# Four weight fetches, one weight split and six one-hot rows change their places in the last quarter of an attention loop

## The chip, the core and the metric
One core of one Trainium2 chip runs one program that does an attention layer and then a mixture-of-experts layer (MoE). The metric is the time of one execution in microseconds (us). TensorE is PE in the profile, VectorE is DVE, ScalarE is ACT, GpSimd is POOL, and SyncE (SP) issues most DMAs.

## The reference
Four batches, eight heads, 768 tokens, head size 64. Per token: attention to the 31 nearest keys (|distance| < 16) and to 24 block summaries of 32 keys each, in one softmax. Keys are summarised by a maximum, values by a mean.

```python
k_sum = k.reshape(B, H, nb, block, D).max(axis=3)
v_sum = v.reshape(B, H, nb, block, D).mean(axis=3)
a = softmax(concat(mask(q @ k.T / 8), q @ k_sum.T / 8 + log(32)))
attn = a @ concat(v, v_sum)
```

The MoE layer takes each token's 512 values. A gate picks one of eight experts by the largest logit; a second logit decides whether a token keeps the expert of the token before it. The output is `p[e] * (relu(x @ w1[e]) @ w2[e])`, with w1[e] 512 x 1024 and w2[e] 1024 x 512.

## The kernel before
**Attention.** Two heads make a pair, so there are 16 pairs, numbered n, four to a batch. Each pair is worked in two groups of three 128-token blocks: 32 groups, numbered G, with n = G // 2. The loop over G is written out in Python, and each engine runs its instructions in the order in which the loop emits them. Group G's scores (`s_mm`, L305 mask matmuls, then L311) come first; then the transposes of group G-2 (`t_stage`, L337, copied out by ACT at L338), the maximum and the exponentials of group G (`s_max` L319, `s_exp` L327), and the weighted sum of group G-3 (`a_mm` L348, scaled by DVE at L359 and L360).

**What GpSimd prepares.** For pair n+1, in pair n's first group, it copies the keys into overlapping windows (`windows`, L269, out `kb`) and folds the values once (`fold_v`, L254, reads the DMA-loaded tile `vt`). In pair n's second group it writes the key summaries into the same `kb` (`summaries`, L272). The scores of pair n+1 need both parts of `kb`. Then it spreads pair n's value summaries into `vw` (`spread_v`, L283).

**What is mixed in.** While attention runs, earlier batches are routed: x is transposed (L553, copied by ACT at L560), logits are made (`x_logits`, L570), and `route` works through small DVE steps with a few matmuls (L644 counts the tokens of each expert from `sc` of L640). The most wanted expert of batch 0, `e0`, is known early, and its weights are fetched during attention: eight chunks of 128 x 1024, 512 KB each, into a rotation of four `wst` buffers (`wfetch`, L1146 on SP). A chunk is split into a rounded part (ACT cast, L1150) and a remainder (`wsplit`: four GpSimd instructions at L1158, or one on DVE at L1153). Chunk 0 is split on GpSimd.

`rows` (L680 to L683) builds six one-hot 128 x 128 tiles of batch 0 on GpSimd from `lanf`; the routing of batch 0 leaves it to the loop, which calls it as `self.set0()` in group SET0.

**The order around the change.** SP issues, in one queue: in the first group of pair n the value loads `vt` of pair n+2 and `vw` of pair n+1; in the second group the keys and queries of pair n+3; weight fetches come behind the loads of their group. Near the end of each group the jobs registered for "point 1" run (L461), then `set0` (L462). The lists are read in `have_e0` (L1400 to L1405):

```python
for j in range(len(WSPLIT)):
    at(WSPLIT[j], 1, wsplit, j)
for j in range(len(WFETCH)):
    at(WFETCH[j], 1, wfetch, j)
```

Chunk 4 reuses chunk 0's buffer, so its fetch in group 26 waits for the end of split 0. After the loop, six more splits and two more fetches follow at fixed points of the tail, and the MoE work begins with the first gathered tokens (L1164, L1175).

Of the kernel before, what the change touches and what calls it, by code (L numbers as in the profile page):

```python
# [50 lines left out]
WARM = 11  # L51
WHOLE = (3, 4, 5)
LATE = (*WHOLE, 9, 13)
SET0 = 25
BEHIND = (5, 16, 24, 30)
SOON = (8, 12)
FILL = {2: 5}

WFETCH = (21, 21, 22, 22, 26, 30)
WSPLIT = (24, 29)  # L60
WBY = "GGGVVVGV"

TAIL = {0: ("t", 30), 1: ("a", 29), 2: ("t", 31), 4: ("a", 30), 5: ("a", 31)}
# [21 lines left out]
class Kernel:  # L85
# [87 lines left out]
    def attention(self, tick, rows, tail):  # L173
        nc, tc, ident = self.nc, self.tc, self.ident
        with ExitStack() as ctx:
# [200 lines left out]
            for G in range(last_g):  # L376
# [84 lines left out]
                tick(G, 1)  # L461
                if G == SET0:  # L462
                    self.set0()
# [913 lines left out]
    def run(self):  # L1377
# [5 lines left out]
        def at(G, point, f, *args):  # L1383
            jobs.setdefault((G, point), []).append((f, args))
# [6 lines left out]
        def wfetch(j):  # L1391
            w, q = divmod(j, NCH)
            st["w", j] = self.awk.tile([P, CH], F32, name="wst", bufs=4)
            self.fetch(st["w", j], w, q * CH, (q + 1) * CH, st["e0"])

        def wsplit(j):
            w, q = divmod(j, NCH)
            self.split(w, q * CH, (q + 1) * CH, st.pop(("w", j)), nc.vector if WBY[j] == "V" else nc.gpsimd)

        def have_e0():  # L1400
            st["e0"] = nc.values_load(self.e0[0:1, 0:1], engines=(ENG.SP,), min_val=0, max_val=E - 1)
# [5 lines that stand above are left out]
# [50 lines left out]
        def tail(stage):  # L1457
# [3 lines left out]
            for k in range(XL[-1] + 4):  # L1461
# [5 lines left out]
                if k in WLAST:  # L1467
                    wsplit(len(WSPLIT) + WLAST.index(k))
                if k in WLATE:
                    wfetch(len(WFETCH) + WLATE.index(k))  # L1470
                for u in range(NU):
# [289 lines left out]
```

## Time and profile before

| what | value |
|---|---|
| time, median of 3 runs | 436.49 us (434.3 to 437.31) |
| profiled execution: time, span | 433.81 us, 432.0 us |
| PE busy | 416.2 us, 96% of the span |
| DVE, ACT, POOL busy | 234.1, 197.5, 165.9 us |
| PE clock granted, mean | 0.99 of full speed |
| HBM traffic | 69.65 MB read, 12.71 MB written |

The span is what the trace covers; the time is what was measured for the execution, 1.8 us more. Attention fills about the first 115 us, the MoE layer the rest. In a timeline row the columns are start, duration, engine, line and operation, then output, inputs, shape and count; a bracket gives the idle time of that engine ahead of the row and who ended it.

### The profile page before, as it was taken

The page shows a single profiled execution, that of the slowest core. Times are in us where ns is not written, and L with a number is a line of the kernel's source. Part 1 is how long each engine was busy: PE and PEld are TensorE (multiplying, and loading weights), DVE is VectorE, ACT ScalarE, POOL GpSimd, SP SyncE. Part 2 cuts the span into 40 slices and gives each one's busy share as a digit, 9 for nine tenths or more (in the row PEclk, how much of TensorE's full clock was granted, in tenths as well). Part 3 has the DMA queues.
Part 4 walks back from the last instruction along what each step waited for, and adds up shares of the span by engine and source line. Part 5 has one row for each costly group of instructions (what it writes and reads, how often), then busy time and mean ns, then how long its engine had stood idle before and what let it go on. Part 6 is the DMA issues. An engine that isn't in the chain of part 4 may idle for free.

```text
span 432.0 us, 11296 instructions
## 1 busy us (share of the span) xinstructions
PE 416.2 (96%) x4227; PEld 360.3 (83%) x4228; DVE 234.1 (54%) x575; ACT 197.5 (46%) x466; POOL 165.9 (38%) x255
## 2 busy tenths in 40 slices
PE   7999999989999999999999999999999999999992
PEld 4787887868898798988987998799899889879781
DVE  4876796978788689957721022112435202254560
ACT  4988887967865227322121222122634212263561
POOL 3667686798624315753022103110630310321131
PEclk9999999989999999999999999999999999999997
DMA  8999999997251850394076912110257210219312
GB/s 310 403 396 402 400 329 377 401 402 284 95 177 68 325 212 0 99 368 170 2 284 231 374 52 72 29 50 0 99 185 255 90 58 0 57 53 388 105 51 58
DMA packets 22279, 83.27 MB, mean 193 GB/s; under 512 B 2702, under 2 KB 3344, under 8 KB 19120
## 3 DMA queue, kind: packets, MB, share of 16 engines
q1 hardware_dynamic: 17600, 67.75, 41.1%
q0 software_dynamic: 4448, 14.29, 10.0%
q8 instruction: 39, 0.64, 0.6%
q14 instruction: 48, 0.39, 0.3%
q10 hardware_dynamic: 144, 0.20, 0.2%
HBM read 69.65 MB, written 12.71 MB: 191 GB/s over the span
## 4 chain that ended last, share of the span: by engine, by line
issue 25%; DMA 12%; POOLq 5%; POOL 4%; PE 3%; DVE 3%; DVEq 0%
DMA out_dram<-yo,sidx 9%; POOLq L1273 4%; POOL xg L1164 2%; DMA out_dram<-few_y,sidx 2%; DMA xg<-x_dram,gidx 1%; DVE bp L1084 1%; POOL l L1158 1%; POOLq L1481 1%; PE bs L1249 1%; PE bt L1111 1%; PE bs L1251 0%; PE bs L1252 0%; DVE hT L1258 0%; DVE eqp L1078 0%; POOL out_dram L1209 0%
## 5 line engine op out<-in xcount | busy, mean ns | idle before, releaser
L1249 PE MATMUL bs<-xT,h 128*128 128x384 f32 (+1 forms) x288 | 91.3, 317 | 0.0
L1251 PE MATMUL bs<-xT,h 128*128 128x384 f32 (+1 forms) x288 | 89.8, 312 | 0.0
L1252 PE MATMUL bs<-xT,l 128*128 128x384 f32 (+1 forms) x288 | 89.7, 311 | 0.0
L1196 PE MATMUL ba<-h,hT 128*128 128x512 f32 x192 | 78.9, 411 | 1.4 <-PEq L1646 0.8
L1258 DVE SCALAR_TENSOR_TENSOR hT<-bs,hT 128x384 fp32r<-128x384 f32 (+1 forms) x56 | 33.2, 593 | 82.9 <-ACT hT L1256 69.2
L1198 PE MATMUL ba<-h,hT 128*128 128x512 f32 x192 | 75.3, 392 | 0.0
L1197 PE MATMUL ba<-l,hT 128*128 128x512 f32 x192 | 75.0, 391 | 0.0
L1256 ACT ACTIVATE hT<-bs 128x384 fp32r<-128x384 f32 (+1 forms) x56 | 29.3, 523 | 86.9 <-PE bs L1252 84.9
L1164 POOL DMA_INDIRECT xg<-x_dram,gidx x30 | 29.4, 981 | 101.5 <-PE bt L1175 90.5
L1249 PEld LDWEIGHTS bs<-xT,h 128*128 128x128 f32 x288 | 54.5, 189 | 0.8 <-issue 0.4
L327 ACT ACTIVATE pr<-bs,nm 128x120 f32<-128x120 f32 x192 | 51.7, 372 | 7.5 <-DVE nm L319 6.9
L1251 PEld LDWEIGHTS bs<-xT,h 128*128 128x128 f32 x288 | 54.5, 189 | 0.4
L1252 PEld LDWEIGHTS bs<-xT,l 128*128 128x128 f32 x288 | 54.5, 189 | 0.0
L1209 POOL DMA_INDIRECT out_dram<-yo,sidx x24 | 28.0, 1168 | 64.4 <-ACT yo L1205 40.9
L1196 PEld LDWEIGHTS ba<-h,hT 128*128 128x128 f32 x192 | 36.2, 189 | 8.7 <-issue 2.6
L1198 PEld LDWEIGHTS ba<-h,hT 128*128 128x128 f32 x192 | 36.0, 188 | 8.2
L1197 PEld LDWEIGHTS ba<-l,hT 128*128 128x128 f32 x192 | 36.2, 189 | 6.0
L1153 DVE TENSOR_TENSOR l<-stg,h 128x1024 fp32r<-128x1024 f32 x28 | 34.4, 1274 | 12.0 <-ACT h L1150 11.9
L1170 DVE TENSOR_TENSOR xT<-bt,xT 128x512 fp32r<-128x512 f32 x27 | 18.6, 691 | 36.5 <-ACT xT L1168 34.3
L1150 ACT CAST h<-stg 128x1024 fp32r<-128x1024 f32 x32 | 32.2, 1049 | 11.4 <-PEq L1646 4.6
L1205 ACT ACTIVATE yo<-ba,psort 128x512 f32<-128x512 f32 x24 | 16.5, 688 | 45.1 <-PE ba L1198 41.5
L283 POOL COPY vw<-vs 24x384 f32<-24x384 f32 x64 | 29.9, 509 | 13.6 <-ACT vs L278 5.4
(269 smaller groups left out, 639.4 us busy)
## 6 DMA issues: line engine op xcount, KB each, us to landing
stg<-in_w SPq DMA_DIRECT2D x16, 1024.0 KB, 7.7
vw<-in_vW SPq DMA_DIRECT2D x16, 780.0 KB, 7.4
few_w<-in_w SPq DMA_DIRECT2D x8, 1024.0 KB, 8.4
kp<-in_kT SPq DMA_DIRECT2D x16, 384.0 KB, 6.9
q<-in_qT SPq DMA_DIRECT2D x16, 384.0 KB, 7.6
vt<-in_vT SPq DMA_DIRECT2D x16, 384.0 KB, 7.0
x_dram<-xs SPq DMA_DIRECT2D x8, 768.0 KB, 5.8
wst<-in_w SPq DMA_DIRECT2D x8, 512.0 KB, 7.4
```

The costliest lines, as they stand in the source:

```text
L283: nc.gpsimd.tensor_copy(out=vw[n % 3][WL:W, t:t + NW // 4, :, 0:D], in_=vs.to_broadcast([NB, NW // 4, 2, D]))
L327: nc.scalar.activation(out=pr[:, h, u, 0:W], in_=sp[:, h, u, :], func=AF.Exp, bias=nm[:, h, u:u + 1], scale=1.0)
L1150: self.nc.scalar.copy(out=hi, in_=src)
L1153: eng.tensor_tensor(out=lo, in0=src, in1=hi.bitcast(F32), op=ALU.subtract)
L1164: self.nc.gpsimd.indirect_dma_start(out=t, out_offset=None, in_=rows, in_offset=bass.IndirectOffsetOnAxis(ap=self.gidx[:, i:i + 1], axis=0))
L1196: nc.tensor.matmul(out=ps, lhsT=ah, rhs=wh, start=first, stop=False)
L1197: nc.tensor.matmul(out=ps, lhsT=ah, rhs=wl, start=False, stop=False)
L1198: self.last_mm = nc.tensor.matmul(out=ps, lhsT=al, rhs=wh, start=False, stop=last).ins
L1249: ins = nc.tensor.matmul(out=ps[:, j], lhsT=wh, rhs=xh[c], start=(c == 0), stop=False).ins
L1251: nc.tensor.matmul(out=ps[:, j], lhsT=wh, rhs=xl[c], start=False, stop=False)
L1252: nc.tensor.matmul(out=ps[:, j], lhsT=wl, rhs=xh[c], start=False, stop=(c == KT - 1))
L1258: nc.vector.scalar_tensor_tensor(out=l, in0=ps, scalar=0.0, in1=h.bitcast(F32), op0=ALU.max, op1=ALU.subtract)
```

## The change
Three constants change. The first four weight chunks are fetched in groups 22, 22, 23 and 23 instead of 21, 21, 22 and 22. The one-hot rows of batch 0 are built in group 24 instead of 25. Chunk 0 is split in group 25 instead of 24. The later fetches (26, 30) and the second split (29) stay.

```diff
-SET0 = 25
+SET0 = 24
...
-WFETCH = (21, 21, 22, 22, 26, 30)
-WSPLIT = (24, 29)
+WFETCH = (22, 22, 23, 23, 26, 30)
+WSPLIT = (25, 29)
```

On GpSimd, the order from group 24 on was: windows and fold of pair 13, split 0, summaries of pair 13, spread of pair 12, one-hot rows. It becomes: windows and fold of pair 13, one-hot rows, summaries of pair 13, spread of pair 12, split 0. On ACT the cast of chunk 0 moves from the end of group 24 to the end of group 25. On SP the four fetches move past the loads of one group: chunks 0 and 1 go behind `vt` of pair 13 and `vw` of pair 12, chunks 2 and 3 behind the keys and queries of pair 14.

## Rows read from the trace of the kernel before

**Rows 1.** Windows: busy us (and instructions) by engine, PE clock, DMA share, GB/s
```profile
80.00:100.00 20.00, 17.91 (x331) 14.80 (x319) 17.05 (x41) 15.54 (x52) 15.74 (x30) 0.91 1.02 396
100.00:120.00 20.00, 20.00 (x354) 17.31 (x348) 16.01 (x52) 15.62 (x48) 13.36 (x24) 1.00 0.44 153
...
200.00:432.00 232.00, 222.46 (x1420) 198.16 (x1418) 79.58 (x127) 71.94 (x113) 48.42 (x45) 0.99 0.33 117
```

**Rows 2.** Waits of PE from 80 to 96 us: total, times, longest
```profile
PE bs L311 <- POOL kb L272: 1.9, 1, 1.9
```

**Rows 3.** Timeline of PE: starts of groups 18, 19, 26, 27; scores and logits
```profile
60.03 0.35 PE L305 MATMUL bs<-me 64*64 64x360 bf16 x4
...
63.73 0.35 PE L305 MATMUL bs<-me 64*64 64x360 bf16 x4
...
88.25 0.35 PE L305 MATMUL bs<-me 64*64 64x360 bf16 x4
90.48 0.85 PE L311 MATMUL bs<-kb,q 64*64 64x120 f32 x24 [1.88 <-POOL kb L272]
...
95.52 0.35 PE L305 MATMUL bs<-me 64*64 64x360 bf16 x4
...
100.04 1.07 PE L570 MATMUL bs<-hs,wg 128*32 128x128 f32 x24
```

**Rows 4.** Timeline of POOL, groups 24 and 25, and one row of group 29
```profile
81.30 1.49 POOL L269 TENSOR_SCALAR kb<-kp 128x384 f32<-128x384 f32 x3
84.85 1.15 POOL L254 TENSOR_TENSOR vf<-vt 128x192 f32<-128x192 f32 x2 [2.06 <-DMA vt<-in_vT]
87.25 2.78 POOL L1158 TENSOR_TENSOR l<-wst,h 128x256 fp32r<-128x256 f32 x4 [1.25 <-ACT h L1150]
89.99 0.43 POOL L272 TENSOR_SCALAR kb<-ks 128x288 f32<-128x288 f32 x1
90.49 1.85 POOL L283 COPY vw<-vs 24x384 f32<-24x384 f32 x4
92.44 3.52 POOL L682 TENSOR_SCALAR A<-c,lanf 128x128 bf16<-128x128 f32 x6
...
104.94 0.43 POOL L272 TENSOR_SCALAR kb<-ks 128x288 f32<-128x288 f32 x1 [0.56 <-DVE tl L853]
```

**Rows 5.** SP's issues; landing times of vt (pair 13), of four weight chunks
```profile
75.79 0.89 SPq L1146 DMA_DIRECT2D wst<-in_w  x2
76.79 0.38 SPq L202 DMA_DIRECT2D vt<-in_vT  x1
...
80.01 0.88 SPq L1146 DMA_DIRECT2D wst<-in_w  x2
...
DMA to landing us min/median/max: 7.9/7.9/7.9
...
DMA to landing us min/median/max: 6.7/7.8/8.9
```

**Rows 6.** Windows, the stretch behind the stall, columns as in the first group
```profile
92.00:95.30 3.30, 3.30 (x37) 3.05 (x34) 1.97 (x5) 2.76 (x9) 3.20 (x6) 0.50 1.02 399
```

**Rows 7.** Timeline of ACT, groups 24, 25 and 27
```profile
86.13 1.04 ACT L1150 CAST h<-wst 128x1024 fp32r<-128x1024 f32 x1
...
87.82 1.62 ACT L327 ACTIVATE pr<-bs,nm 128x120 f32<-128x120 f32 x6
...
97.05 0.86 ACT L338 COPY pt<-bt 124x384 f32<-124x384 f32 x2 [0.84 <-PE bt L337]
...
99.41 1.05 ACT L560 COPY hs<-bt 128x512 f32<-128x512 f32 x2
```

**Rows 8.** Timeline of DVE: routing steps of batch 1, one of batch 2
```profile
89.40 0.65 DVE L632 TENSOR_SCALAR e_all<-ev 128x6 int32<-128x6 int32 x1
...
90.51 0.59 DVE L640 TENSOR_TENSOR_SCAN sc<-c,oh 128x48 bf16<-128x48 f32 x1
...
125.65 0.16 DVE L632 TENSOR_SCALAR e_all<-ev 128x6 int32<-128x6 int32 x1
```

## The prediction
> **What bounds the kernel now.** I read the busy time by stretches first [rows 1]. From 100 us on PE is busy in all or nearly all of each stretch, while between 80 and 100 us it is busy for 17.91 of 20.00 us, its granted clock is 0.91, and the DMA engines are full (share 1.02, 396 GB/s). So the kernel is bound by PE, with a hole just where the edit lies. Next came the waits of PE there: one matters, the scores waiting for GpSimd's key summaries, 1.9 us, once [rows 2]. Then the timeline of PE around it [rows 3]: group 26 starts at 88.25, its L311 only at 90.48, and group 27 at 95.52, so group 26 lasts 7.27 us. Group 18, which has the same mixture (a pair's first group, two blocks of x transposed), lasts 63.73 - 60.03 = 3.70 us. The excess is 3.57 us, and two things make it up. The wait is 1.88. Behind it the granted clock is 0.50, the lower level of 1.2 GHz, for 3.30 us [rows 6], which costs half of that, 1.65 us. Together 3.53: the hole is explained.
>
> Last I followed GpSimd back from that wait [rows 4]. Ahead of the summaries at 89.99 stand, from the back: split 0 (2.78 us), 1.25 us of waiting for ACT's cast of chunk 0, the fold (1.15 us), and 2.06 us of waiting for the `vt` load of pair 13. That load was issued at 76.79, right behind two weight chunks at 75.79, and landed after 7.9 us, at 84.7 [rows 5].
>
> **The change, part by part.**
>
> *Fetches.* Chunks 0 and 1 go behind `vt`: 2 x 512 KB = 1.05 MB at 396 GB/s [rows 1] is 2.65 us of transfer that no longer stands ahead of it. If the queue serves in order of issue, `vt` lands near 84.7 - 2.65 = 82.05. GpSimd is free at 81.30 + 1.49 = 82.79 [rows 4], so the 2.06 us of waiting goes and the fold runs from about 82.8 to 83.95. Chunks 0 and 1 now go out where 2 and 3 did, at 80.01 and just after, and land 6.7 to 8.9 us later [rows 5], at 86.7 to 89.4. Chunks 2 and 3 move one group on; they are split only in the tail, past 115 us, which hides them. The loads passed by them land earlier or as before. Issuing costs SP the same 0.89 us per two, so its queue holds nothing new.
>
> *Rows and split on GpSimd.* In the place of the 1.25 us wait and the 2.78 us split come the six rows, 3.52 us, whose input was finished long before: 83.95 + 3.52 = 87.5, plus 0.43 for the summaries = 87.9. PE asks for them at about 88.4. The wait of 1.88 us should be gone with 0.5 us to spare, and with it the cause of the clock's fall. The spread follows (1.85 us) to 89.8, then split 0 once cast. Fetch 4 waits for split 0's end, near 93.3 instead of 90.0; it was issued only at 97 before, so SP loses nothing.
>
> *Next on GpSimd.* Split 0 ends near 90.5 + 2.78 = 93.3; windows, fold and summaries of pair 14 (1.49, 1.15, 0.43) end at 96.4. Group 28's L311 ran one L311 (0.85 us) before L570, at about 99.2 [rows 3]; 96.4 permits it 2.8 us earlier.
>
> *ACT.* The cast (1.04 us) leaves group 24 and lands behind the exponentials of group 25. Those end at 87.82 + 1.62 = 89.44 [rows 7], or up to 0.67 sooner, since the copy behind the cast could start when its transposes were done. In order from there: cast 1.04, copy 0.86, exponentials 1.62, two hs copies 1.05, copy 0.86, exponentials 1.62, a small copy of about 0.25, and half of 1.05 for the hs tile that L570 of group 28 needs. That is 7.8 us: ready at 97.3, or 96.6. Against 100.04 the gain is 2.7 to 3.4. Before, ACT idled through the stall, and that idle time hid such work; now it doesn't. PE alone would have arrived 3.57 earlier, at 96.5, so up to 0.8 us of the prize is given back here and on GpSimd; the two lie beside each other and count once.
>
> *DVE.* The routing steps before L644 end at 90.51 + 0.59 = 91.10 [rows 8]. PE used to be stalled; now it comes to L644 near 89.9. The same step L632 took 0.65 us with GpSimd working and 0.16 with it idle [rows 8]. At the short durations there is no wait; if the steps still end at 91.1, PE waits 1.2 us, group 27 starts at 93.15 and L570 at 97.7, a gain of 2.4.
>
> The Trainium skill, GPSIMD Engine Reference, section 8 (Key points), says that GpSimd shares its SBUF interfaces with VectorE and contends with DVE instructions in a two-port mode or with two SBUF inputs. By that rule the long durations stay, as GpSimd is still busy there (the spread), and the sum would be 2.4; by the idle-GpSimd row it would be 2.7 or more.
>
> *Carried to the end.* PE is busy in 20.00 of 20.00 us from 100 to 120, and in 222.46 of 232 after 200 [rows 1]; the gathers, splits and later fetches are issued by steps that follow the same loop, so they move with it. The nearest thing to a fixed date is the last pairs' loads, as the DMA engines are full until about 102 us: the last `vt` can't come 3 us earlier. But GpSimd's summaries of pair 15 at 104.94 waited for DVE and not for a load [rows 4], and they run some 2 to 3 us before group 30 asks. I carry the gain whole.
>
> *Sum.* Ends 2.4 and 3.4, I take 2.9 us: 433.81 - 2.9 = 430.9 for the profiled execution. That one lies 2.68 below the median of the three runs (436.49), so the median to expect is **433.6 us**, 0.7% less.
>
> **The rivals.**
> 1. *The load does not come earlier* (the DMA queue does not serve in order, or the load was late for another reason). For: the landing times alone don't prove an order. Against: chunks take 6.7 to 8.9 us in a full queue, growing as they queue up [rows 5]. Then the fold still ends at 86.0, the rows at 89.5, the summaries at 89.95: 0.5 us better, the stall and the low clock stay. Time 436.0. Chance 0.14. The Trainium skill, DMA: Bandwidth & Descriptors, Queues, rings and completion order, says that completion is not first-in-first-out per issuing engine, which is this rival's mechanism; no run here shows yet which holds for these loads.
> 2. *The stall goes or shrinks to under 1 us, but the clock falls anyway* in group 26 or 27, because PE still meets short waits there. It costs the 1.65 us again: gain 1.3, time 435.2. For: the fall came 1.5 us after the wait had ended. Against: at no other place of the attention did a short wait bring it. Chance 0.13.
> 3. *More than the hole:* the runs shown are 0.5 to 3.5 us longer than the profiled one; if they lose that in a longer stall at this place, the gain is about 5, time 431.5. Nothing in the profile speaks for the place. Chance 0.06.
> 4. *Slower: the cast of chunk 0 holds ACT.* ACT runs in order; it now meets the cast 3 us later, but the chunk is issued 4.2 us later. From a landing past about 89 us ACT stands still, and past 92.4 the split delays pair 14's summaries beyond the old 99.2, each us counting fully, plus 1.65 if the clock falls. A landing at 95.5 would cost 3.1 + 1.65 = 4.8, time 441. Against: it takes 15.5 us for a load where 8.9 is the longest of the four. Chance 0.05.
>
> That the lists do what they say is plain from how they are read.
>
> **How the numbers follow.** Forecast 0.62, rivals 0.14, 0.13, 0.06, 0.05. A measurement of this kernel tells about 1% from no change, 4.36 us. The forecast and rivals 1 and 2 lie within it, except where the medians scatter: the three runs span 3.0 us, which may push a gain of 2.9 past 4.36. I put 0.13 of the forecast and all of rival 3 there: faster 0.19. Slower is rival 4 and a trace of scatter, 0.06. Same 0.75. The range takes the forecast's ends (gain 2.4 to 3.4) with 2 us of scatter below, and reaches to rival 1 above: 430.8 to 436.7. The forecast's own range is 431.5 to 435.
>
> **What would show it.** L311 of group 26 without a wait for L272; granted clock 1.00 from 92 to 96; the fold of pair 13 at 82.8 with no DMA wait ahead; group 26 about 3.7 to 4.9 us long; L570 of group 28 near 97.1. Wrong would be: the fold still at 84.8 (rival 1), a 0.50 clock with no stall (rival 2), ACT idle ahead of the cast (rival 4), or a gain at group 28 that is gone by 200 us.

## The result and the profile after

The changed kernel took **431.21 us** (median of 7 runs, 430.94 to 435.22), the kernel before 435.77 (7 runs, 434.3 to 437.31). The medians lie 4.56 us apart; the ratio, which goes by all the runs, gives less: 0.9919, 95% interval [0.9892, 0.9947], 0.8% or some 3.5 us. A repetition on another chip (below, `e4_after_again`) gave 0.9927 [0.9904, 0.9951]. So it is faster by 0.7 to 0.8%, and both intervals exclude 1.

A profile shows one execution: those of the kernel before, of `e4_after_again` and of `e7` are the shortest of their kernel's runs, and the first one of the changed kernel and those of `e3`, `e6` and `e8` are the longest. So the first profile of the changed kernel (435.22 us, span 433.4) has to be read with care. Its windows show a PE that is busy for less of the stretch than before [rows 1], though the granted clock no longer falls [rows 6]:

```profile
80.00:100.00 20.00, 15.85 (x311) 13.12 (x303) 16.71 (x43) 14.96 (x50) 16.02 (x31) 1.00 0.99 365
92.00:95.30 3.30, 1.58 (x32) 1.24 (x31) 2.91 (x7) 1.25 (x4) 3.19 (x7) 1.00 1.02 393
```

The timeline of PE in it shows why. L311 follows L305 at once in group 26, as forecast; but PE now stands still twice at other places:

```profile
90.27 0.45 PE L348 MATMUL ba<-vw,pt 124*64 124x65 f32 x6 [1.94 <-issue]
90.64 0.35 PE L305 MATMUL bs<-me 64*64 64x360 bf16 x4
90.82 0.79 PE L311 MATMUL bs<-kb,q 64*64 64x120 f32 x24
94.13 0.18 PE L644 MATMUL bt<-sc,cb 128*128 128x8 bf16 x1 [1.72 <-DVE sc L640]
96.18 0.35 PE L305 MATMUL bs<-me 64*64 64x360 bf16 x4
...
100.70 1.07 PE L570 MATMUL bs<-hs,wg 128*32 128x128 f32 x24
```

The 1.94 us are put down to "issue", nothing that the profile shows. L570 of group 28 comes at 100.70, later than the 100.04 of before [rows 3]. A second profile of the same kernel, which came with `e4_after_again`, shows an execution of 430.09 us, span 428.3. All statements on the change rest on that one. Its windows:

```profile
80.00:100.00 20.00, 19.39 (x382) 15.97 (x375) 19.02 (x48) 17.73 (x58) 18.59 (x36) 1.00 1.01 377
92.00:95.30 3.30, 3.30 (x67) 2.73 (x66) 3.23 (x10) 3.08 (x10) 3.30 (x7) 1.00 0.97 357
```

PE is busy for 19.39 of 20.00 us where it was 17.91, and in the stretch that had run at half clock it issues 67 matmuls where it had issued 37. The timeline of PE, against [rows 3]:

```profile
87.62 0.35 PE L305 MATMUL bs<-me 64*64 64x360 bf16 x4
87.87 0.84 PE L311 MATMUL bs<-kb,q 64*64 64x120 f32 x24
90.14 0.18 PE L644 MATMUL bt<-sc,cb 128*128 128x8 bf16 x1 [0.61 <-DVE sc L640]
92.19 0.35 PE L305 MATMUL bs<-me 64*64 64x360 bf16 x4
95.99 0.79 PE L311 MATMUL bs<-kb,q 64*64 64x120 f32 x24
96.71 1.15 PE L570 MATMUL bs<-hs,wg 128*32 128x128 f32 x24
```

Group 26 lasts 92.19 - 87.62 = 4.57 us (7.27 before), and L570 of group 28 starts 3.33 us earlier (100.04 - 96.71). Of these, 2.70 us are made in group 26, 0.48 in group 25 (2.84 us instead of 3.32; before, PE stopped there for 0.21 us with nothing to wait for, see the last section), and 0.15 ahead of group 22. Group 27 lasts 3.63 us in both. From L570 to the end of the span it takes 428.3 - 96.71 = 331.6 us, before 432.0 - 100.04 = 332.0. So nearly the whole gain is made ahead of L570, and nothing is given back.

The timeline of GpSimd, against [rows 4]:

```profile
81.19 1.49 POOL L269 TENSOR_SCALAR kb<-kp 128x384 f32<-128x384 f32 x3
82.77 1.15 POOL L254 TENSOR_TENSOR vf<-vt 128x192 f32<-128x192 f32 x2
83.90 3.52 POOL L682 TENSOR_SCALAR A<-c,lanf 128x128 bf16<-128x128 f32 x6
87.39 0.44 POOL L272 TENSOR_SCALAR kb<-ks 128x288 f32<-128x288 f32 x1
87.88 1.85 POOL L283 COPY vw<-vs 24x384 f32<-24x384 f32 x4
89.84 2.84 POOL L1158 TENSOR_TENSOR l<-wst,h 128x256 fp32r<-128x256 f32 x4
92.64 1.47 POOL L269 TENSOR_SCALAR kb<-kp 128x384 f32<-128x384 f32 x3
94.06 1.17 POOL L254 TENSOR_TENSOR vf<-vt 128x192 f32<-128x192 f32 x2
95.18 0.45 POOL L272 TENSOR_SCALAR kb<-ks 128x288 f32<-128x288 f32 x1
...
102.28 1.15 POOL L254 TENSOR_TENSOR vf<-vt 128x192 f32<-128x192 f32 x2 [2.30 <-DMA vt<-in_vT]
```

From the windows of pair 13 to the end of the summaries of pair 14 there is hardly any idle time left: 95.63 - 81.19 = 14.44 us. Before, the same nine pieces of work took from 81.30 [rows 4] to 98.93, that is 17.63 us, with 2.06 + 1.25 = 3.31 us of waiting in them. Their end, in the kernel before:

```profile
98.50 0.43 POOL L272 TENSOR_SCALAR kb<-ks 128x288 f32<-128x288 f32 x1
```

This chain became 3.19 us shorter, and PE's way from the start of group 22 to L570 of group 28 3.18 us (23.41 to 20.23).

### The profile page after: what moved, and what is told of

The parts are those of the page before. It is cut to its first block, busy times and chain, and to the rows that moved or that the text cites. A ratio compares the mean times of both kernels' runs of the same rounds, so it can differ in the third digit from the quotient of the medians.

```text
span 433.4 us, 11296 instructions
## 1 busy us (share of the span) xinstructions
PE 414.5 (96%) x4228; PEld 359.2 (83%) x4228; DVE 234.0 (54%) x575; ACT 197.6 (46%) x466; POOL 164.4 (38%) x255
```

## The experiments

Theory: the fold's wait for `vt` (2.06 us) and the split's wait for ACT's cast (1.25 us) both stand in GpSimd's chain, and both edits are needed to take them out. The rivals: the earlier fetch alone does it; the swap alone does it; the clock's fall is what costs. The first four kernels ran together on one chip, where the kernel before had 434.80 (33 runs).

**The fetches alone** (kernel before with one line changed).

```diff
-WFETCH = (21, 21, 22, 22, 26, 30)
+WFETCH = (22, 22, 23, 23, 26, 30)
```

> Only the four fetches move (groups 22, 22, 23, 23); split 0 stays in group 24, the rows in group 25. Theory A (the stall ahead of group 26 is the sum of a late vt load and of the split with its wait for ACT, so both parts of the change are needed): vt of pair 13 lands near 82.2 and the fold is done by 84, but chunk 0 is now issued at 80.0 and lands at 86.6 to 88, so ACT stands at its cast from about 86.2, the split ends near 90.5 and the summaries near 90.9; the stall of 1.9 us stays or grows by up to 0.6: ratio to the kernel before 0.998 to 1.003. Theory B (the load of vt alone made the stall): summaries near 88, ratio 0.990 to 0.993.

Measured: 433.86 us, ratio 0.9986 [0.9971, 1.0002], no difference that can be told. GpSimd's timeline, then one row of PE's:

```profile
84.30 1.14 POOL L254 TENSOR_TENSOR vf<-vt 128x192 f32<-128x192 f32 x2 [0.95 <-DVE va L247]
...
88.66 2.77 POOL L1158 TENSOR_TENSOR l<-wst,h 128x256 fp32r<-128x256 f32 x4 [3.22 <-ACT h L1150]
91.40 0.43 POOL L272 TENSOR_SCALAR kb<-ks 128x288 f32<-128x288 f32 x1
```

```profile
91.88 1.17 PE L311 MATMUL bs<-kb,q 64*64 64x120 f32 x24 [2.40 <-POOL kb L272]
```

The wait for `vt` is gone from the fold, as it should be (`vt` landed near 81.5; the 0.95 us are a wait for DVE, which still reads the tile of the fold before); the split then waits 3.22 us instead of 1.25, and the summaries come at 91.40, later than the 89.99 of before [rows 4]. PE's wait grew to 2.40 us, and L570 of group 28 came 24.37 us behind group 22 (23.41 before). In one detail my expectation failed. ACT did not stand still for the chunk; the cast ran at 87.55 directly behind other work of ACT (the exponentials of group 25 and a copy):

```profile
85.93 1.68 ACT L327 ACTIVATE pr<-bs,nm 128x120 f32<-128x120 f32 x6
87.40 0.24 ACT L278 COPY vs<-bt 24x128 f32<-24x128 f32 x1
87.55 1.04 ACT L1150 CAST h<-wst 128x1024 fp32r<-128x1024 f32 x1
```

So the split waited for the cast's place in ACT's order, not for the data.

**The swap alone** (kernel before).

```diff
-SET0 = 25
+SET0 = 24
-WSPLIT = (24, 29)
+WSPLIT = (25, 29)
```

> Only the rows (group 24) and split 0 (group 25) change places; the fetches stay in groups 21 and 22. Theory A: vt of pair 13 still lands at 84.7, the fold ends at 86.0, the rows at 89.5, the summaries at 89.95: PE still waits about 1.5 us for them and the clock may fall as before; ratio 0.996 to 1.000. Theory C (the order on GpSimd, freed of ACT's cast, is what counts, and the load does not matter): ratio 0.990 to 0.993.

Measured: 433.31 us, 0.9967 [0.9951, 0.9982], under half of the gain. The late fold now stands in front of the rows (`vt` landed near 84.2; the fold starts at 84.42, with 1.67 us of idle time ahead of it), and the summaries come at 89.03, sooner than I expected (89.95). PE still waits for them, and again at group 28:

```profile
89.51 0.85 PE L311 MATMUL bs<-kb,q 64*64 64x120 f32 x24 [0.63 <-POOL kb L272]
...
98.03 0.85 PE L311 MATMUL bs<-kb,q 64*64 64x120 f32 x24 [0.92 <-POOL kb L272]
```

The clock keeps 1.00 from 92 to 95.3 here, and L570 of group 28 comes 22.34 us after group 22 starts (98.81 - 76.47); before it was 23.41 (100.04 - 76.63), in the changed kernel 20.23 (96.71 - 76.48). Not all of the difference lies behind group 25: groups 22 to 25 took 12.1 us in the profiles of `e1`, `e2` and `e3`, against 11.62 before and 11.14 in the changed kernel, as PE waits twice at L348 in each of the three, for 0.30 to 0.42 us. Why is not shown.

**The changed kernel with the rows put back** (rows behind the split again, in group 25).

```diff
-SET0 = 24
+SET0 = 25
```

> Fetches late and split 0 in group 25 as in the changed kernel, but the rows stay in group 25, behind split 0. Theory A: summaries of pair 13 come right behind the fold, at 86.5 to 87, so no stall at group 26; but rows (3.5 us) and split (2.8 us) now both lie ahead of the windows of pair 14, whose summaries end near 100, and PE waits 0.5 to 1 us at group 28 (asked for at about 96 to 99): of the changed kernel's gain little is left, ratio 0.995 to 1.000. Theory D (only what lies ahead of pair 13's summaries matters): the full gain, ratio 0.989 to 0.992.

Measured: 436.07 us, 1.0032 [1.0016, 1.0047]. Expected was no loss; the loss tells most of the four. The rows, which are no work that group 26 needs, now stood between split 0 and the windows of pair 14, and the stall appeared at the next pair, longer than the 0.5 to 1 us that I expected there:

```profile
102.20 1.48 PE L311 MATMUL bs<-kb,q 64*64 64x120 f32 x24 [4.22 <-POOL kb L272]
```

PE's clock was 0.50 behind it (102 to 106 us). The stall is not tied to group 26; it is GpSimd's debt, which is paid at the next summaries that PE needs. GpSimd also stood idle for 2.30 us ahead of the summaries of pair 13, waiting for DVE (which had just finished `ks`, L243), and for 1.27 us ahead of the split. In the changed kernel the rows fill that time.

**The changed kernel again**, unchanged.

> The changed kernel once more, unaltered, for a second profile of it. The first profiled execution was the slowest of seven (435.22 against a median of 431.21) and shows PE stopped for 1.94 us inside group 25's weighted sum with no instruction to wait for. Theory A: an ordinary execution lacks most of that stop and shows L311 of group 26 near 88 with no wait for L272, group 28 some 3 us or more earlier than before; time 430.9 to 432.6, ratio 0.989 to 0.992. Rival: the stop is in every execution and the gain comes from elsewhere, then the profile again shows about 1.9 us there.

Measured: 431.13 us, 0.9927 [0.9904, 0.9951]. The ratio missed what was expected by a little, the time did not. PE's 1.94 us stop of the first profile is absent in this one.

**Filling the stall, so that the clock stays up** (kernel before; eight dummy matmuls ahead of group 26's scores). This was to measure the clock's share by itself.

```diff
-FILL = {2: 5}
+FILL = {2: 5, 26: 8}
-                    warm(FILL[G], "a")
+                    warm(FILL[G], "a" if G == 2 else "t")
```

> The kernel before, plus eight dummy matmuls (128x512, about 0.21 us each, 1.7 us) on PE ahead of group 26's scores, where PE stands still anyway; their output is not used. It prices the clock's fall apart from the wait. Theory A (the wait costs 1.9 us and the fall of the clock behind it another 1.65 us, because PE stood still): L311 of group 26 still starts when the summaries are done, near 90.5, but the clock stays at 1.00 from 92 to 96 and group 27 starts 1.4 to 1.7 us sooner: ratio to the kernel before 0.995 to 0.998. Rival E (the fall has no part in the lost time, or comes whatever PE does in the wait): ratio 1.000 to 1.004.

Measured: 437.85 us, 1.0064 [1.0040, 1.0087], slower, against my expectation. The clock did stay up: granted 1.00 from 92 to 95.3 us, with 65 matmuls. PE's timeline (it has seven of the eight dummies):

```profile
88.35 1.90 PE L222 MATMUL bt<-wz 128*128 128x512 bf16 x7
...
91.10 0.84 PE L311 MATMUL bs<-kb,q 64*64 64x120 f32 x24 [0.57 <-POOL kb L272]
94.62 0.35 PE L305 MATMUL bs<-me 64*64 64x360 bf16 x4
...
100.33 0.85 PE L311 MATMUL bs<-kb,q 64*64 64x120 f32 x24 [1.73 <-POOL kb L272]
...
409.49 0.39 PE L1196 MATMUL ba<-h,hT 128*128 128x512 f32 x1 [1.46 <-issue]
```

Group 27 starts 17.41 us behind group 22 (94.62 - 77.21); before it was 18.89 (95.52 - 76.63). So 1.48 us of the clock's 1.65 were saved there. At group 28 PE waits 1.73 us for the summaries of pair 14, and L570 is no sooner: 23.90 us behind group 22 against 23.41. **The clock's share was not worth anything by itself**, since GpSimd's chain ended at 98.93 before, only 0.39 us ahead of PE's L311 of group 28:

```profile
99.32 0.79 PE L311 MATMUL bs<-kb,q 64*64 64x120 f32 x24
```

Of the 1.73 us, 0.70 have another source: the fold of pair 14 took 1.85 us in `e5` instead of 1.15, at the same time as a one-hot instruction of DVE (L689, 1.44 us instead of 0.96). The rest of the loss is in the tail; the kernels with the rows on DVE, below, come back to it.

**The fetches two groups later still** (changed kernel): how far rival 4 of the prediction is.

```diff
-WFETCH = (22, 22, 23, 23, 26, 30)
+WFETCH = (24, 24, 25, 25, 26, 30)
```

> The changed kernel with the four fetches two groups later still (24, 24, 25, 25). It tests the slower rival of the prediction: ACT meets the cast of chunk 0 before the chunk is there. If DMAs are served in order of issue, chunk 0 stands behind vt of pair 14 and vw of pair 13 and lands near 90.5 to 92; ACT waits 2 to 3 us ahead of the cast, split 0 ends near 95, the summaries of pair 14 near 98, and PE waits 1 to 2.5 us at group 28. From L305 of group 22 to L570 of group 28 it takes 22 to 23.5 us (changed kernel 20.2, kernel before 23.4): ratio 0.995 to 1.000. If order of issue does not matter, the chunk lands within 6 to 7 us of its issue all the same and the ratio is that of the changed kernel, 0.991 to 0.994.

Measured: 434.71 us, 0.9997 [0.9980, 1.0013]: the gain is gone. The profile is of an execution of 440.56 us and shows the mechanism only; that an execution of 434.71 loses the gain in the same way is not shown. Chunk 0 was issued at 89.05 and landed about 8.5 us later. The cast holds ACT, and the split holds GpSimd; first ACT's row, then GpSimd's, then PE's:

```profile
97.54 1.04 ACT L1150 CAST h<-wst 128x1024 fp32r<-128x1024 f32 x1 [4.74 <-DMA wst<-in_w]
```

```profile
98.72 2.77 POOL L1158 TENSOR_TENSOR l<-wst,h 128x256 fp32r<-128x256 f32 x4 [4.95 <-ACT h L1150]
```

```profile
99.01 1.97 PE L553 MATMUL bt<-ident,xs 128*128 128x128 f32 x8 [3.74 <-ACT pt L338]
```

PE waits for the copy behind the cast, still in group 26, and not for the summaries of pair 14. L570 of group 28 came 26.68 us behind group 22, where I had expected 22 to 23.5.

**Chunks 2 and 3 out of the way** (changed kernel): is the last `vt`, which the fold of pair 15 waits 2.30 us for, worth anything?

```diff
-WFETCH = (22, 22, 23, 23, 26, 30)
+WFETCH = (22, 22, 27, 27, 28, 30)
```

> The changed kernel with chunks 2 and 3 fetched in group 27 and chunk 4 in group 28, behind most loads of the attention. In the second profile of the changed kernel the next thing late is the fold of pair 15, 2.3 us of waiting for its vt load at 102.3, which PE does not feel. Theory A (PE is the bound there, the load hidden): the wait of the fold shrinks to under 0.5 us and the time is that of the changed kernel, ratio to the kernel before 0.991 to 0.994. Rival F (the full DMA queue holds the rest of attention back): another 1 to 2 us faster, ratio 0.987 to 0.990.

Measured: 430.57 us, 0.9909 [0.9887, 0.9931], not to be told from the change (0.9927 [0.9904, 0.9951]). The fold's wait fell from 2.30 to 0.55 us, and L570 came 20.18 us behind group 22 (20.23): nobody had waited for that fold.

**The rows on DVE** (kernel before; the rows of batch 0 leave GpSimd), then **the same with the fill**, then **the fill in group 26 in the place of the one in group 2**. If GpSimd's chain was what took the fill's gain, the fill should be worth 1 us or more at group 28 once GpSimd has less to do. And the third kernel has the same number of PE instructions up to the scores of group 26 as the kernel before, where `e5` has 16 more (eight matmuls and their weight loads).

```diff
-        if b == 0:
-            self.set0 = rows
-        else:
+        self.set0 = lambda: None
+        if True:
```

> The kernel before with the one-hot rows of batch 0 built by DVE in one instruction (0.96 us) in the routing, as the other batches' are; GpSimd loses 3.5 us of work in group 25. In the runs so far the time from L305 of group 22 to L570 of group 28 follows GpSimd's idle time between pair 13's windows and pair 14's summaries (before 23.4 us with 3.3 idle, changed kernel 20.2 with none, e1 24.4, e2 22.3, e3 25.7). Theory G (two paths of nearly equal length end at group 28 in the kernel before: GpSimd's chain, summaries of pair 14 done at 98.9, and PE's own, the wait plus the slow clock, at 99.3): relieving GpSimd alone leaves PE's path, 22.9 to 23.5 us, ratio 0.998 to 1.001. Rival H (GpSimd's chain alone sets it): 20 to 20.5 us, ratio 0.991 to 0.994.

> The kernel of e8 with the eight dummy matmuls of e5 ahead of group 26's scores (their output is not used). Theory G: with GpSimd off the path and the clock kept at 1.00, group 28 now starts sooner, L305 of group 22 to L570 of group 28 in 21.6 to 22.3 us, 1.4 to 1.7 below e8, the price of the clock alone. The whole time still carries the 2.9 us that e5 lost after 400 us: ratio 1.001 to 1.004 against e5's 1.0064. Rival: the same 23.4 to 23.9 us as e5, then neither GpSimd nor the clock is the reason.

```diff
-FILL = {2: 5}
+FILL = {26: 5}
-                    warm(FILL[G], "a")
+                    warm(FILL[G], "t")
```

> The kernel before with the five dummy matmuls of group 2 moved to group 26 (their output is not used in either place), so that PE's instructions behind group 26 stand at the same count as in the kernel before. In e5, which adds 16 instructions to PE, PE stopped 1.46 us at 409 us with nothing to wait for and ran at half clock behind it. Theory I (PE stops where a block of its instructions comes late, so the place depends on the instruction count): the stop at 409 is gone, from L570 of group 28 to the end 331 to 332.5 us (e5 334.9, before 332.0); ratio 0.997 to 1.003. Rival J (the dummies themselves do it, through bank order or timing): again about 334.9 us, ratio 1.004 to 1.008.

Measured, against 435.99 us of the kernel before (33 runs): rows on DVE 437.77, 1.0038 [1.0018, 1.0057]; with the fill 438.33, 1.0052 [1.0027, 1.0077]; the fill moved 438.33, 1.0043 [1.0021, 1.0065]. As times the first and the third missed, the second by a little. The stretches that I had put down missed as well: from group 22 to L570 `e8` took 25.15 us (22.9 to 23.5 expected) and `e9` 22.88 (21.6 to 22.3), and `e10` took 333.9 us from L570 to the end (331 to 332.5). What they show in their traces:

- With the rows off GpSimd the filled kernel no longer waits at group 28, and L570 comes 22.88 us behind group 22, 1.02 sooner than the 23.90 of `e5`; counted from the start of group 26, which comes 0.94 later in `e9`, it is 1.96 sooner. That is what the chain on GpSimd had swallowed.
- The kernel with the rows on DVE and no fill was already 3.7 us late at group 19 in its profile (67.41 against 63.73), ahead of any effect of the rows on group 26; PE waits 1.67 us for GpSimd's summaries at 29.07. `e9` and `e11`, with the same rows on DVE, are only 0.6 and 0.2 us late there, so it is not the rows. That profile can't price the rows, and why the kernel's time is higher stays open.
- Both kernels with the eight dummies have a stop of PE with no releaser shown in the tail, 1.46 us at 409.49 and 1.81 us at 409.99; the kernel before, the changed one and the one with the fill moved have none there. Counted from group 29's start, the rest of the run takes 330.8 and 330.6 us in those two and 326.8 to 329.2 in all others. After the stop of `e5` the granted clock from 410 to 414 us was 0.60; after the other it was 1.00.
- The third lost time at the start, from which it takes the dummies of group 2: over the first 20 us PE's granted clock is 0.91 (1.00 before) and PE waits once 2.0 us for ACT's exponentials (0.9 before).

**Both changes and the rows on DVE** (changed kernel; chunks as in `e7`; the rows as in `e8`): a version that could beat the change.

```diff
-SET0 = 24
+SET0 = 25
-WFETCH = (22, 22, 23, 23, 26, 30)
+WFETCH = (22, 22, 27, 27, 28, 30)
...
-        if b == 0:
-            self.set0 = rows
-        else:
+        self.set0 = lambda: None
+        if True:
```

> A candidate that takes the change's split place and the fetches of e7 and builds the rows on DVE as in e8. Theory G: with the change GpSimd is no longer what PE waits for, so taking 3.5 us more from it gives PE nothing: L305 of group 22 to L570 of group 28 in 19.8 to 20.3 us, ratio to the kernel before 0.989 to 0.994, like the changed kernel. Rival: 1 us or more below it, 0.986 to 0.989.

Measured: 433.75 us, 0.9954 [0.9936, 0.9972], less than the change gains. L570 came 22.42 us behind group 22, where I had expected 19.8 to 20.3. GpSimd has 3.52 us less to do, but its summaries for group 26 now wait 2.30 us for DVE:

```profile
88.24 0.43 POOL L272 TENSOR_SCALAR kb<-ks 128x288 f32<-128x288 f32 x1 [2.30 <-DVE vm L620]
```

PE did not feel that wait itself: the summaries end at 88.67, and group 26 starts at 89.64. The loss lies ahead of it and behind it. Groups 22 to 25 took 12.86 us (11.14 in the changed kernel), with three waits of PE at L348 of 0.41 to 0.64 us that the profile puts down to DVE, and L311 of group 28 waits 0.82 us for the summaries of pair 14. Whether the rows on DVE cause the first is not shown.

No version beat the changed kernel.

## Why the prediction was nearly right, and where it was not

**The time (inside the range, in part by luck).** 431.21 us lies in the stated range of 430.8 to 436.7, but 0.3 us below the forecast's own 431.5 to 435; only the 2 us of scatter below hold it. By the prediction's own terms the lower bound is 433.1 - 2 = 431.1 and not 430.8, which the measured time still meets. The mechanism was right in its main steps, as follows.

**The order of the loads (right).** I took it that the queue serves in order of issue, and `vt` near 82.05. In the changed kernel's second profile `vt` was issued at 75.97 and landed 5.8 us later, at 81.8, before GpSimd was free at 82.68; the fold ran at 82.77 (82.8 foretold) with no wait. Rival 1 is refuted, by `e1` as well. Taking 1.05 MB from in front of this load brought it 2.9 us earlier (84.7 to 81.8), where order of issue asked for 2.65; 0.8 us of that is that SP issued it sooner (75.97 instead of 76.79), 2.1 that it took 5.8 us to land instead of 7.9. The Trainium skill (DMA: Bandwidth & Descriptors, Queues, rings and completion order) says that completion is not first-in-first-out per issuing engine; here the traces of the kernel before, of the changed kernel, of `e1` and of `e2` show no overtaking: the loads that SP issued between 75 and 83 us landed in the order of their issue.

**Rows and split (right).** Rows to 87.42 (87.5 foretold), summaries to 87.83 (87.9), PE asks at 87.87 and shows no wait; of the 0.5 us to spare almost nothing was left, as PE came sooner than the 88.4 that I took. The clock is 1.00 from 92 to 95.3: rival 2 is refuted for this profile, and `e2` too kept the clock with a wait of 0.63 us left.

**ACT (right, at its early end).** I had the exponentials of group 25 end at 89.44 or up to 0.67 sooner, and from there 7.8 us to L570: 97.3 or 96.6. The cast began at 88.61, right behind them, and L570 at 96.71:

```profile
87.14 1.63 ACT L327 ACTIVATE pr<-bs,nm 128x120 f32<-128x120 f32 x6
88.61 1.09 ACT L1150 CAST h<-wst 128x1024 fp32r<-128x1024 f32 x1
```

**The sum (two terms mis-sized).** I chose 2.9 between 2.4 and 3.4, all of it out of the hole in group 26. Measured were 3.33 at L570, 3.2 by the repetition (434.80 x 0.0073), 3.5 by the first comparison (435.77 x 0.0081). Group 26 alone gave 2.70: it stayed 0.87 us longer than the 3.70 of group 18, and PE's one wait in it, 0.61 us, was for DVE and not for ACT or GpSimd. The other 0.63 us came ahead of group 26, where I had put nothing. That the sum is so near is luck to this extent. The larger miss is the step from the profiled execution to the median: I added 2.68 us, from three runs, and measured it is 1.12 (430.09 to 431.21). That is 1.6 of the 2.4 us by which 431.21 lies below the forecast of 433.6; the profiled execution (430.9 forecast) makes the other 0.8.

**DVE (between its ends).** L632 took 0.43 us, between the 0.16 beside an idle GpSimd and the 0.65 of before [rows 8], beside the spread on GpSimd:

```profile
88.88 0.43 DVE L632 TENSOR_SCALAR e_all<-ev 128x6 int32<-128x6 int32 x1
89.82 0.26 DVE L640 TENSOR_TENSOR_SCAN sc<-c,oh 128x48 bf16<-128x48 f32 x1
```

PE waited 0.61 us for the scan (0 to 1.2 foretold), and group 26 took 4.57 us (3.7 to 4.9). In `e1`, beside the split, L632 took 0.63, and in `e3`, beside an idle GpSimd, 0.17. The rule of the Trainium skill (GPSIMD Engine Reference, section 8) that the two engines contend in a two-port mode or with two SBUF inputs agrees in sign, though no run shows in which mode L632 works; the sum it gave, 2.4, was too low.

**Carried whole (right).** 331.6 us from L570 to the end, 332.0 before. The fold of pair 15 did wait for its load, by 2.30 us, and `e7` shows that PE did not feel it.

**"The hole is explained" (right in its sum, wrong in its reading).** I added a wait of 1.88 and a clock loss of 1.65 on PE as if each were a prize of its own. `e5` took away the second alone (dummies filled the first): group 27 came 1.48 us sooner, L570 of group 28 no sooner. `e3` put the rows elsewhere, and the stall went to group 28. What sets L570 is the longer of two chains, PE's (with its stall and low clock) and GpSimd's in groups 24 to 27, and the two ended 0.39 us apart. In eight profiles (before, `e1` to `e5`, `e7`, `e10`) GpSimd's chain from the windows of pair 13 to the end of the summaries of pair 14 takes 14.4 to 19.4 us, and PE's way from group 22 to L570 is 5.6 to 6.2 us longer in each. In `e9`, with the rows off GpSimd, it is 8.8 us longer (22.88 and 14.11): there PE's own chain is the longer one. My price was near because the edit takes 3.2 us out of both at the same time; I had listed pair 14's summaries as "2.8 us earlier" only as a permission, where they are half of the reason.

**Each part needs the other (not foretold).** `e1` gains nothing that can be told, `e2` 0.3%, both together 0.7 to 0.8%. An early `vt` alone moves GpSimd sooner to a split whose cast has not been made; the rows alone wait behind a late fold. Put together, the fold ends at 83.92, and rows, summaries and spread (5.8 us) fill the time until ACT has cast (88.61 + 1.09 = 89.70).

**Rival 4 (not met; its mechanism was right, its place not).** With the fetch two groups later (`e6`) ACT stood still 4.74 us for the chunk, and the whole gain went; but in its profile PE lost the time to ACT's copy in group 26, not to the summaries of pair 14. **Rival 3 (not met, in part open).** In the profile the gain is 3.3, not 5, and the two intervals, 2.3 to 4.7 and 2.1 to 4.2 us, exclude 5. But the time came out near its 431.5, and the medians lie 4.56 and 3.67 us apart; where they gain more than the profile shows is open.

**Open:** why the kernels with the rows on DVE are slower, what the waits at L348 in groups 22 to 25 come from, and what the stops of PE in the last section hang on.

## What to carry to other kernels

Where an engine stalls, add up the work and the idle time of the engine that it waits for, from one delivery to the next but one: what a fix is worth is about the smaller of what it takes off the waiting engine and off its supplier. (Here `e5`, which relieved PE alone, shows it; `e8`, which was to relieve GpSimd alone, could not.) Of an in-order engine's queue, put work whose input is long there into the gap ahead of work that still waits for another engine, and check at the next delivery that the debt is not only deferred.

## What the runs showed of the hardware

PE stops with nothing to wait for, beside small packets of a queue that the profile calls "instruction". In the first profile of the changed kernel such a packet moved between 87.75 and 88.00 us, and PE, which stood for 1.94 us, went on at 90.27. The row of the queue in that window (packets, MB, share of the window):

```profile
q8 instruction: 1, 0.02, 25.4%
```

In the kernel before the packet came in 85.25 to 85.50, and PE stopped at the same instruction (18 of the 24 L348 of that group were done) for 0.21 us only:

```profile
87.88 0.45 PE L348 MATMUL ba<-vw,pt 124*64 124x65 f32 x6 [0.21 <-issue]
```

In the second profile of the changed kernel it came at 84.5 to 85.0, and there was no stop. In `e5` it came in 407 to 408, and PE went on at 409.49. In each of the three with a stop PE goes on 1.5 to 2.6 us behind the packet. That suggests that PE waits there for the next block of its program; that reading is only argued. The packet alone is not enough: the kernel before has one in 406 to 407 and `e10` one in 408 to 409, without a stop. Nor are full DMA engines needed: their share was 0.15 around the stop of `e5` (406 to 410). Why the packet comes 2.5 us later in one execution than in another stays open. The two kernels with 16 more PE instructions both have a stop at about 409 us, and the one with as many as before has none.

The clock's fall does not follow each stop: in the kernel before it was 0.50 after a wait of 1.88 us, in `e1` 0.54 after 2.40 (both from 92 to 95.3 us) and in `e3` 0.50 after 4.22, while after stops of 1.94 and 1.72 us in the first profile of the changed kernel it stayed 1.00.

The fold of pair 14 on GpSimd took 1.84 to 1.94 us in `e2`, `e3`, `e5` and `e10`, where DVE's one-hot instruction L689 ran at the same time, and 1.15 to 1.17 before, in the changed kernel and in `e7`, where it did not; L689 took 1.34 to 1.44 us in `e3`, `e5` and `e10` and 0.94 to 0.96 in the other four. So work that is moved on one of the two engines can cost time on the other.
